# One-hot moves of 16 rows, and transposes of three more head pairs on VectorE and DMA, in a fused attention and feed-forward kernel

## The chip, the cores and the metric

The kernel runs on one core of a Trainium2 chip (trn2). The metric is the device time of one execution in microseconds (us). Each kernel was executed several times, and medians are quoted; one of the executions was also recorded with the hardware profiler, and all lines of profiles below come from those recorded executions. An execution of a one-core kernel counts as slow when it is over 1.5% above the fastest of the same kernel; comparisons use fast runs.

Engines in the profile: PE is TensorE (matmuls; PEld its weight loads), DVE is VectorE, ACT is ScalarE, POOL is GpSimd, SP is SyncE, which only issues DMAs here (SPq is its sequencer). L220 is line 220 of the kernel that was profiled, so the same statement has other line numbers in other kernels. Of the tile names, QK are the prepared q and k, ohT the one-hot rows, S the scores, pT their exps, VX the prepared v, OB the accumulator of the output, M a bank of PSUM (the memory that TensorE writes), Tq the blocks transposed on VectorE and T the same data after it has been put in place.

## The reference

Attention with routing: every query and every key is assigned to the nearest of 16 cluster centroids of its head, and a query sees only the keys of its own cluster. The result goes through a feed-forward layer with the activation h + sin²(αh)/α.

```python
# q, k, v: (4 batches, 8 heads, 768 tokens, 64); centroids: (8, 16, 64); float32
q_assign = argmax(einsum('bhsd,hcd->bhsc', normalized(q), normalized(centroids)), -1)
k_assign = argmax(einsum('bhsd,hcd->bhsc', normalized(k), normalized(centroids)), -1)
mask = q_assign[:, :, :, None] == k_assign[:, :, None, :]
scores = where(mask, q @ k.T / sqrt(64), -1e9)
attn = softmax(scores)
x = (attn @ v) as (3072 tokens, 512)
h = x @ w_in                       # (512, 2048)
g = h + sin(alpha * h)**2 / (alpha + 1e-9)
out = g @ w_out                    # (2048, 512)
```

## The kernel before

The work is cut into 16 pairs of heads: pairs 0 to 3 are batch 0, and so on. For each batch, 48 attention steps (12 a pair) are followed by 16 blocks of the feed-forward layer, called the MoE stretch below. An attention step is one block of 128 keys by 768 queries of one head: two matmuls for the scores, one exp on ScalarE, and six matmuls of an earlier step's weights with V.

The mask costs no vector work: below the 64 rows of q and k lie 16 rows that hold the one-hot cluster of each token, and one row with +1 for q and −1 for k, so that a score gets an addition only within a cluster. So each pair has to be prepared in time: q and k transposed (tokens to columns), cast to bf16, multiplied by the centroids (the "cluster product", on TensorE), made one-hot on VectorE, and moved by DMA to rows 64 and up.

There are two ways to transpose. `prep_T` uses TensorE, and VectorE copies the result out. `prep_D` transposes 32×32 blocks on VectorE, and `prep_S` then places the blocks with eight DMAs of 96 KB; I call these eight a placing. Each engine gets its instructions in one fixed order; a dictionary `plan` says at which step a piece of the preparation is put into the instruction streams. The parts that matter:

```python
    NPE = 2 * NHP          # pairs 0..7 are transposed on TensorE, 8..15 by prep_D, prep_S
    ...
    def prep_S(m):         # a placing: 8 DMAs, all from SyncE's queue
        s = st[m]
        s["T32"] = trp.tile([P, 4, HS], F32, tag="T32", name="T32")   # trp has 2 buffers
        for i in range(4):
            for e in range(2):
                lo = D * (i // 2) + 32 * e
                nc.sync.dma_start(
                    out=s["T32"][lo : lo + 32, :, QS * (i % 2) : QS * (i % 2) + QS],
                    in_=s["Tq"][32 * i : 32 * i + 32, :, QS * e : QS * e + QS],
                )
    ...
    def prep_asn(m, bk=None):        # cluster product: 4 fp32 products, 8 matmul passes
        ...
        for g in range(4):
            nc.tensor.matmul(out=bk[32 * g : 32 * g + 32, 0:HS],
                lhsT=cnB[:, 2 * hp + g // 2, :], rhs=s["T32"][:, g, :], start=True, stop=True)
    ...
    def prep_move(m):                # one-hot rows and the sign row: 17 rows
        ...
            nc.sync.dma_start(
                out=QK[D:KR, m % NQK, h, t],
                in_=s["ohT"][32 * g : 32 * g + NHC + 1].rearrange("c a n -> c (a n)"),
            )
    ...
    def prep(m, s0):
        if m == 1:
            s0 -= 4
        else:
            for g in range(4):
                if m < NPE:
                    if m != NHP + 3 or g == 3:
                        at(s0 + g, lambda g=g: prep_T(m, g))
                else:
                    at(s0 - 5 + g, lambda g=g: prep_D(m, g))
            if m >= NPE:
                at(s0 - 2, lambda: prep_S(m))
                s0 += STEPS          # STEPS is 12: the consumers come a pair later
            at(s0 + 2, lambda: prep_cast(m, 0))     # GpSimd
            at(s0 + 4, lambda: prep_cast(m, 1))
        at(s0 + 5, lambda: (prep_asn(m), prep_hot(m, 0)))
        at(s0 + 6, lambda: (prep_hot(m, 1), prep_hot(m, 2)))
        at(s0 + 7, lambda: (prep_hot(m, 3), prep_move(m)))
    # ... weights of the MoE: GpSimd issues these 512 KB loads in its own order
    for i, fn, n in ((23, load_w_in, 0), (30, load_w_out, 0), (36, load_w_in, 1), (42, load_w_in, 2),
                     ...four more at step 47):
```

The softmax here doesn't subtract the row's maximum and nothing guards it: scores larger than these inputs give would overflow.

## Time and profile before

The median is 327.9 us (327.72 to 328.38, 3 runs). The profiled execution spans 327.7 us. The page's share of busy time, its TensorE clock and DMA rows (40 equal slices of the span, in tenths) and its DMA packets:

```profile
PE 307.2 (94%) x2744; PEld 183.0 (56%) x2787; DVE 208.0 (63%) x361; ACT 241.8 (74%) x325; POOL 112.3 (34%) x181
...
PEclk9889999999999999999999999999999999999999
DMA  7455498993016959723043948520043210000031
...
DMA packets 25298, 37.83 MB, mean 115 GB/s; under 512 B 2852, under 2 KB 19120, under 8 KB 25264
```

Batch 0 takes slices 2 to 8. The DMA row is at about half in slices 2 to 5 (8 to 41 us).

Batch 0 is 2.1 us longer than batch 1, with more TensorE work; an undisturbed exp starts 0.71 to 0.73 us after the one before, so 48 of them would take about 35 us. The timeline of TensorE in batch 0 shows the work that the change is about (start, duration, engine, line, operation):

```profile
43.55 0.52 PE L143 MATMUL M<-ident_f,k 128*128 128x128 f32 x3
...
45.27 0.85 PE L211 MATMUL M<-T,cnB 128*32 128x384 f32 x8
```

The first is one of the transposing groups of `prep_T`, the second a cluster product: it makes its step about 1.4 us long.

In the first MoE stretch TensorE waits a little for the output weights, and over the whole execution GpSimd waits long for placings (total us, times, longest):

```profile
PE OB L360 <- DMA w_out_bf<-in_moe_w_out_dram: 0.7, 2, 0.3
...
POOL QK L190 <- DMA T<-Tq: 88.6, 10, 30.8
```

### The profile page before, as it was taken

To read this page: it belongs to the slowest core of one execution; us is meant where nothing else is said; L and a number is where in the kernel's file an instruction comes from. 1 tells how busy PE (TensorE), PEld (TensorE's weight loads), DVE (VectorE), ACT (ScalarE), POOL (GpSimd) and SP (SyncE) were. 2 spreads that over 40 slices of the span, in tenths; PEclk is the share of its full clock that TensorE was granted. 3 is DMA by queue.
4 is the path that set the end of the run, shared out by engine and by line. 5 is a ranking of instruction groups with operands and counts; after the bars stand their busy time and mean duration, and the time that the engine had idled before them with its cause. 6 is when DMAs were issued, how large, how long until landed. Compare 5 with 4: busy or idle time off the path is not lost.

```text
span 327.7 us, 7166 instructions
## 1 busy us (share of the span) xinstructions
PE 307.2 (94%) x2744; PEld 183.0 (56%) x2787; DVE 208.0 (63%) x361; ACT 241.8 (74%) x325; POOL 112.3 (34%) x181
## 2 busy tenths in 40 slices
PE   6699999899999999999999998999999999999995
PEld 3266665555555655555555565655555666555544
DVE  4578887487837556587837766677836613577721
ACT  5288888777678988687778887787779899688300
POOL 7858787620007069280005366340006200000000
PEclk9889999999999999999999999999999999999999
DMA  7455498993016959723043948520043210000031
GB/s 230 139 174 167 137 201 184 209 215 108 10 64 181 233 108 247 222 61 132 2 116 93 233 108 245 143 85 2 0 113 88 60 44 34 0 35 0 0 127 67
DMA packets 25298, 37.83 MB, mean 115 GB/s; under 512 B 2852, under 2 KB 19120, under 8 KB 25264
## 3 DMA queue, kind: packets, MB, share of 16 engines
q0 software_dynamic: 8704, 19.93, 24.0%
q1 hardware_dynamic: 16346, 17.39, 18.6%
q8 instruction: 22, 0.36, 0.5%
q14 instruction: 12, 0.10, 0.1%
q10 hardware_dynamic: 214, 0.06, 0.1%
HBM read 27.30 MB, written 6.29 MB: 103 GB/s over the span
## 4 chain that ended last, share of the span: by engine, by line
PE 56%; DMA 15%; DVE 7%; ACT 7%; POOL 5%; issue 4%; SPq 3%; ACTq 0%; POOLq 0%; DVEq 0%
PE S L389 14%; PE M L360 11%; PE S L313 7%; DMA w_out_bf<-in_moe_w_out_dram 7%; ACT pT L319 6%; PE M L389 6%; DMA k<-in_k_dram 4%; PE OB L328 4%; PE OB L360 4%; DMA T<-Tq 4%; PE S L314 3%; PE M L211 3%; PE S L360 2%; SPq L175 2%; POOL QK L185 2%
## 5 line engine op out<-in xcount | busy, mean ns | idle before, releaser
L319 ACT ACTIVATE pT<-S 128x768 bf16<-128x768 f32 x192 | 145.3, 810 | 27.4 <-PE S L314 25.0
L360 PE MATMUL M<-w_out_bf,gT 128*128 128x512 bf16 (+1 forms) x259 | 82.1, 372 | 0.6 <-DVE asT L243 0.3
L313 PE MATMUL S<-QK 81*128 81x512 bf16 x192 | 73.7, 384 | 7.1 <-POOL QK L185 3.4
L389 PEld LDWEIGHTS <-w_in_bf 128*128 128x128 bf16 x512 | 49.6, 98 | 38.6 <-issue 2.8
L328 PEld LDWEIGHTS <-pT 128*128 128x128 bf16 x1152 | 55.7, 98 | 24.6 <-DVE xs L340 3.5
L389 PE MATMUL S<-xT,w_in_bf 128*128 128x512 bf16 (+1 forms) x348 | 65.0, 325 | 1.1 <-DVE gT L409 0.5
L190 POOL TENSOR_SCALAR QK<-T 64x384 bf16<-64x384 f32 x64 | 33.3, 520 | 94.2 <-DMA T<-Tq 88.6
L328 PE MATMUL OB<-VX,pT 128*128 128x65 bf16 x1152 | 61.0, 194 | 1.9 <-DVE xs L340 1.8
L400 ACT ACTIVATE s_sb<-S,alpha_col 128x768 bf16<-128x768 f32 x44 | 39.4, 902 | 25.3 <-PE S L389 16.2
L360 PEld LDWEIGHTS <-gT 128*128 128x128 bf16 x400 | 39.0, 98 | 28.2 <-issue 2.0
L314 PE MATMUL S<-QK 81*128 81x256 bf16 x192 | 52.2, 272 | 0.0
L409 DVE SCALAR_TENSOR_TENSOR gT<-u_sb,ralpha,S 128x768 bf16<-128x768 bf16 x44 | 44.5, 1013 | 11.2 <-ACT u_sb L405 8.3
L185 POOL CAST QK<-T 64x768 bf16<-64x768 f32 x32 | 26.5, 829 | 43.8 <-DVE T L149 35.9
L314 PEld LDWEIGHTS <-QK 81*128 81x128 bf16 x192 | 18.9, 99 | 22.2 <-issue 7.7
L389 PE MATMUL M<-xT,w_in_bf 128*128 128x512 bf16 (+1 forms) x156 | 29.7, 324 | 0.7 <-DVE gT L409 0.5
L407 DVE TENSOR_TENSOR u_sb<-s_sb 128x768 bf16<-128x768 bf16 x40 | 23.7, 593 | 8.5 <-ACT s_sb L400 8.3
L313 PEld LDWEIGHTS <-QK 81*128 81x128 bf16 x192 | 18.8, 98 | 16.2 <-issue 11.2
L339 DVE RECIPROCAL rec<-OB 128x6 f32<-128x6 f32 x32 | 5.9, 186 | 32.9 <-PE OB L328 32.9
L400 ACT ACTIVATE s_sb<-M,alpha_col 128x512 bf16<-128x512 f32 (+1 forms) x40 | 21.0, 575 | 7.8 <-PE M L389 7.8
L409 DVE SCALAR_TENSOR_TENSOR gT<-u_sb,ralpha,M 128x512 bf16<-128x512 bf16 (+1 forms) x40 | 22.8, 611 | 5.9 <-ACT u_sb L405 5.4
L360 PE MATMUL OB<-w_out_bf,gT 128*128 128x512 bf16 (+1 forms) x76 | 24.6, 356 | 0.7 <-DMA w_out_bf<-in_moe_w_out_dram 0.7
L405 ACT ACTIVATE u_sb<-s_sb 128x768 bf16<-128x768 bf16 x24 | 20.2, 843 | 0.8
(82 smaller groups left out, 262.5 us busy)
## 6 DMA issues: line engine op xcount, KB each, us to landing
T<-Tq SPq DMA_DIRECT2D x64, 96.0 KB
out_dram<-o_sb SPq DMA_DIRECT2D x23, 256.0 KB
v<-in_v_dram POOLq DMA_DIRECT2D x14, 384.0 KB, 4.8
q<-in_q_dram POOLq DMA_DIRECT2D x13, 384.0 KB, 6.0
k<-in_k_dram POOLq DMA_DIRECT2D x13, 384.0 KB, 6.8
w_in_bf<-in_moe_w_in_dram POOLq DMA_DIRECT2D x4, 512.0 KB, 11.8
w_out_bf<-in_moe_w_out_dram POOLq DMA_DIRECT2D x4, 512.0 KB, 18.8
QK<-ohT SPq DMA_DIRECT2D x60, 25.5 KB
```

The source lines that it names most:

```text
L185: nc.gpsimd.tensor_copy(out=QK[0:D, m % NQK, h, :, HS * par : HS * par + HS], in_=src)
L190: nc.gpsimd.tensor_scalar(out=QK[0:D, m % NQK, h, t].rearrange("c (n i a) -> c i n a", i=4, a=32)[:, 2 * par : 2 * par + 2], in0=src[:, t] ...
L313: nc.tensor.matmul(out=dst[:, 0:512], lhsT=lhsT, rhs=T[:, 0, 0:512], start=True, stop=True)
L314: nc.tensor.matmul(out=dst[:, 512:S], lhsT=lhsT, rhs=T[:, 0, 512:S], start=True, stop=True)
L319: nc.scalar.activation(out=pT, in_=area(i)[:, 0:S], func=ACTF.Exp, scale=escale)
L328: nc.tensor.matmul(out=o3[:, j, :], lhsT=pT[:, P * j : P * j + P], rhs=VX[m % NVX][:, h, jof(m // NHP, kt), :], start=(kt == 0 and j == 0) ...
L360: nc.tensor.matmul(out=bk[:, lo:hi], lhsT=gT[:, f, P * mt : P * mt + P], rhs=w_out_bf[:, f, lo:hi], start=(f == 0), stop=(f == NF - 1),)
L389: nc.tensor.matmul(out=ar[lo // 512][:, 0 : hi - lo] if isinstance(ar, tuple) else ar[:, lo:hi], lhsT=lhsT, rhs=xT[:, kk, lo:hi], start=(k ...
L400: nc.scalar.activation(out=s_sb[:, lo:hi], in_=src, func=ACTF.Sin, scale=alpha_col[:, f : f + 1])
L405: nc.scalar.activation(out=u_sb, in_=s_sb, func=ACTF.Square)
L407: nc.vector.tensor_tensor(out=u_sb, in0=s_sb, in1=s_sb, op=ALU.mult)
L409: nc.vector.scalar_tensor_tensor(out=gT[:, f, lo:hi], in0=u_sb[:, lo:hi], scalar=ralpha[:, f : f + 1], in1=src, op0=ALU.mult, op1=ALU.add,)
```

## The change

Its intent: (1) move 16 one-hot rows instead of 17, with the constant sign row written once, so that the DMA can be spread over all 16 DMA engines; (2) take the transposes of pairs 4 to 6 off TensorE in batch 0, the costliest attention stretch; (3) halve the cluster products of batch 0 over two steps; (4) put VectorE's pieces one to a step, away from the steps in which it must free the output accumulator; (5) issue the loads of q and k for pairs 8 to 10 in the first MoE, behind a small copy ("pacer") that waits for a point in the MoE. The core of the diff:

```diff
-    NPE = 2 * NHP
+    NPE = NHP
+    MIX = NHP + 3                       # pair 7: still on TensorE, in the first MoE
...
             nc.sync.dma_start(
-                out=QK[D:KR, m % NQK, h, t],
-                in_=s["ohT"][32 * g : 32 * g + NHC + 1].rearrange("c a n -> c (a n)"),
+                out=QK[D : D + NHC, m % NQK, h, t],
+                in_=s["ohT"][32 * g : 32 * g + NHC].rearrange("c a n -> c (a n)"),
             )
...
+    for t in range(2):                  # sign rows, once, in the prologue
+        nc.sync.dma_start(
+            out=QK[D + NHC : KR, :, :, t, :].rearrange("c s h n -> c (s h) n"),
+            in_=sgn[:, t, :].unsqueeze(1).to_broadcast([1, 2 * NQK, S]),
+        )
...
+    def hot_steps(m, a):
+        asn_at.add(a)
+        if a < ASTEPS:
+            at(a - 1, lambda: prep_asn(m, 0, 2))
+            at(a, lambda: (prep_asn(m, 1, 2), prep_hot(m, 0)))
+        else:
+            at(a, lambda: (prep_asn(m), prep_hot(m, 0)))
+        at(a + 1, lambda: prep_hot(m, 1))
+        at(a + 2, lambda: prep_hot(m, 2))
+        at(a + 3, lambda: (prep_hot(m, 3), prep_move(m)))
...
+    def prep_new(m, k0):
+        for g, d in enumerate((-10, -9, -7, -6)):
+            at(k0 + d, lambda g=g: prep_D(m, g))
+        at(k0 - 5, lambda: prep_S(m))
+        at(k0 + 5, lambda: prep_cast(m, 0))
+        at(k0 + 6, lambda: prep_cast(m, 1))
+        hot_steps(m, k0 + 8)
...
+    for m, k0 in {4: 24, 5: 33, 6: 42}.items():
+        prep_new(m, k0)
+    for m, i in {3: 0, 4: 0, 5: 8, 6: 16, 7: 40}.items():
+        at(i, lambda m=m: load_qk(m, eng=nc.gpsimd))
...  # pairs 8 and up: prep_new(m, ASTEPS * b + STEPS * n)
...  # v loads of pairs 5 and up: 26 steps ahead instead of 14
...  # output matmuls of the MoE, used as filler, keep out of all product steps
+            if b == 0 and f == 8:
+                nc.gpsimd.tensor_copy(out=pacer, in_=gT[0:1, f - 2, 0:1])
+                for m in late:
+                    load_qk(m, eng=nc.gpsimd)
```

## The prediction

> **What bounds it now.** The page gives PE 94% busy, ACT 74%, DVE 63%. By the starts of the exps (timeline, ScalarE) I cut the 327.7 us into: prologue 14.1; attention of the four batches 44.6, 42.5, 43.0, 40.3; the MoE stretches after the first three 32.1, 31.5, 31.0; the last MoE and output 48.8. The MoE pitch is 1.73 us per 128 hidden units: TensorE-bound, not to be had. In attention the floor is ScalarE: exps that wait for nothing start every 0.71 to 0.73 us, 48 x 0.72 = 34.6 us a batch. Batch 0 lies 10 us above it:
> - a step with three fp32 transposes (L143) has a pitch of 0.87, 0.15 over the floor; 20 of them, about 3 us;
> - a step with a cluster product (L211, eight matmuls, 0.78 to 0.85 us) takes about 1.4, 0.7 over; six, about 4 us;
> - the rest: PV waiting for VectorE to free OB (one step of 1.66 us, one of 1.27), first steps, x transposes.
>
> **One-hot moves.** The Trainium skill (DMA: Bandwidth & Descriptors, Queues, rings and completion order) says that a copy is spread over the largest number of engines up to 16 that divides its outer size; 17 rows go to one. The trace agrees: such a move leaves 17 packets and one 4-byte completion packet, a 128-partition load 16. The moves issued at 58 to 61 us trickle until about 79 us; DMA share falls from 1.2 to 0.1 at 76 us, yet the last weights land at 81.4 and 83.9: one engine lags. Sixteen rows remove that. In the prologue, moves of 34 packets (0.65 us each, serial) end just before the first scores (13.55 us): I expect these 0.5 to 1 us earlier.
>
> **Pairs 4 to 6.** 36 of batch 0's transposes go. VectorE is even (twelve 0.54 us transposes for twelve 0.55 us evacuations). GpSimd casts grow from 3.3 to 4.2 us a pair. Placing adds 3 x 0.77 MB, about 3.7 us of 16 engines each (packets of 768 B, 58 ns). Loads come earlier, and the DMA was half idle from 16 to 40 us, so weights should not be later than now.
>
> **Halved products.** 0.43 us fits a step's slack; about 0.35 saved on each of four pairs. Pair 6's product moves to batch 1, which gets five instead of three.
>
> **Later batches.** New places avoid the step in which VectorE frees OB: steps of 1.46 to 1.53 should become 0.9, those of 1.34 about 1.06, of 1.74 to 1.80 about 1.4. Batch 3 has one product less, and takes three more output matmuls.
>
> **Sum (estimates from these durations), us saved:** prologue 0.7; batch 0 4.2 (to 40.4); first MoE 0.6 (weight waits of 0.66 and a load wait of 0.35 go, one more transposing group of 0.36 comes); batch 1 0.4; second MoE 0.4; batch 2 1.7; batch 3 0.9; end 0.5. Together 9.4; I take off 0.9 for new VectorE and GpSimd queues in batch 0 (80 to 90% busy there by these counts). Nearly all is on the critical path, as ScalarE idles there.
>
> **Predicted: 319.4 us**, 8 times in 10 within 315.5 to 324.0. Chances: faster by over 2% 0.72, within 2% 0.26, slower 0.02.
>
> **Right if** batch 0's exps span 39 to 42 us, no MoE matmul waits for weights, moves show 16 completion packets, the tail at 76 to 84 us is gone, batch 2 spans about 41. **Wrong if** the first MoE waits for w_out or w_in (placing and loads collide), if PV in batch 0 waits over a microsecond for OB, or GpSimd, blocked on a placing, issues weights late. Then only batches 2 and 3 gain: about 324.

One correction to its wording: the rule for the number of engines stands, in the Trainium skill's page "DMA: Bandwidth & Descriptors", in the section "Why a DMA increments its semaphore by 16 and not by 1", not in the section that the prediction names.

## More of the kernel before

Note for later that a pair that is placed by DMA had its placing at step `s0 - 2` and its cast and product at `s0 + 14` and `s0 + 17`: 16 and 19 steps behind.

The span cut at the exps that begin and end each attention stretch. Columns are: window, its length, busy us (and instructions) of PE, PEld, DVE, ACT and POOL, then the granted TensorE clock, the DMA share and GB/s. The lines are batch 0, the first MoE, batch 1 and batch 2:

```profile
14.11:58.66 44.55, 41.79 (x501) 27.95 (x503) 33.90 (x64) 37.12 (x48) 34.43 (x45) 0.96 0.66 170
58.66:90.79 32.13, 29.98 (x183) 16.98 (x185) 23.61 (x34) 23.38 (x33) 5.56 (x8) 1.00 0.64 127
90.79:133.24 42.45, 40.56 (x464) 24.95 (x472) 24.64 (x49) 36.22 (x48) 21.88 (x34) 1.00 0.65 170
...
164.71:207.69 42.98, 41.14 (x469) 24.66 (x477) 27.90 (x54) 35.97 (x48) 19.67 (x34) 1.00 0.63 163
```

The same cut for 16 to 40 us, and from 41 us to the end of batch 0, shows a DMA share of 0.49 and then 0.91:

```profile
16.00:40.00 24.00, 22.61 (x275) 15.67 (x274) 19.68 (x38) 19.50 (x26) 16.73 (x23) 0.96 0.49 150
41.00:58.66 17.66, 16.39 (x207) 11.20 (x206) 13.22 (x25) 15.10 (x20) 14.89 (x20) 1.00 0.91 198
```

## The result, and the profile after

The changed kernel takes 338.53 us (median of 4 runs, 337.31 to 339.68) against 327.81 (4 runs) before. The ratio is 1.033 (95% interval 1.029 to 1.037): slower. Ratios here and below are the mean time of one kernel's fast runs over that of the other's of the same rounds, so they are not quite the ratio of the medians. The results were correct.

The same parts of the page, after:

```profile
PE 308.8 (92%) x2742; PEld 181.8 (54%) x2783; DVE 205.5 (61%) x360; ACT 242.9 (72%) x326; POOL 116.8 (35%) x188
...
PEclk9989978999999996999999999999999999999999
DMA  7464968989733586592105385632011000000022
...
DMA packets 29746, 40.14 MB, mean 119 GB/s; under 512 B 4264, under 2 KB 23568, under 8 KB 29712
```

The clock row has two dips that were not there, in slices 6 and 7 and in slice 16. The packets under 512 B rise by 1412, from 2852 to 4264: a move leaves 16 completion packets now instead of one (1028 of the rise, as a run below shows), and the other 384 are 16 for each of the 24 DMAs of the three new placings. The stages (batch 0, first MoE, batch 1, batch 2, as before):

```profile
14.35:62.26 47.91, 40.78 (x489) 26.42 (x489) 29.99 (x60) 36.96 (x48) 31.40 (x47) 0.89 0.76 188
62.26:94.50 32.24, 29.95 (x186) 17.16 (x188) 23.19 (x34) 23.76 (x34) 18.26 (x27) 1.00 0.95 224
94.50:143.67 49.17, 43.91 (x478) 25.48 (x485) 31.32 (x59) 36.56 (x48) 23.08 (x38) 0.93 0.55 141
...
174.66:217.89 43.23, 40.68 (x470) 24.43 (x477) 29.00 (x55) 36.27 (x48) 17.31 (x31) 1.00 0.57 139
```

Batch 0 has lost one us of TensorE work and is 3.36 us longer; batch 1 is 6.72 us longer. These two make 10.1 us of a difference of 9.2 in the spans; the other stages differ by half a us or less. So the loss has to be found in two places, and TensorE's timeline shows the first:

```profile
41.97 0.27 PE L327 MATMUL S<-QK 81*128 81x256 bf16 x1
42.07 0.35 PE L341 MATMUL OB<-VX,pT 128*128 128x65 bf16 x6
45.55 0.53 PE L220 MATMUL M<-T,cnB 128*32 128x192 f32 x8 [3.13 <-DMA T<-Tq]
46.02 0.39 PE L326 MATMUL S<-QK 81*128 81x512 bf16 x1
...
47.30 0.87 PE L220 MATMUL M<-T,cnB 128*32 128x192 f32 x8 [0.78 <-DMA T<-Tq]
48.09 0.61 PE L326 MATMUL S<-QK 81*128 81x512 bf16 x1
```

The bracket is the idle time before an instruction and what ended it. The first half product of pair 4 comes up 8.5 us after the first issue of that pair's placing (42.42 and 33.91 us) and waits 3.13 us for it, and the scores of the next step stand behind it in TensorE's order. The next product takes 0.87 us instead of 0.53, and the scores 0.61 instead of 0.39: the clock is at half from 46.4 to 53.3 us.

When was the placing issued, and why does it land so late? First SyncE's issues, then GpSimd in the same time:

```profile
33.91 5.67 SPq L176 DMA_DIRECT2D T<-Tq  x8
39.67 5.06 SPq L300 DMA_DIRECT2D QK<-ohT  x4
```

```profile
35.40 0.77 POOL L615 DMA_DIRECT2D w_in_bf<-in_moe_w_in_dram  x1
44.37 1.07 POOL L197 TENSOR_SCALAR QK<-T 64x384 bf16<-64x384 f32 x2 [8.20 <-DMA QK<-ohT]
47.33 3.66 POOL L197 TENSOR_SCALAR QK<-T 64x384 bf16<-64x384 f32 x6 [1.89 <-DMA T<-Tq]
51.05 0.81 POOL L621 DMA_DIRECT2D w_out_bf<-in_moe_w_out_dram  x1
```

Eight issues take 5.67 us. Beside them go the loads of q, k and v that GpSimd issued just before, and 512 KB of w_in, issued at 35.40. The fourth of the eight lands at 44.21, the last at 47.16: 13.3 us after the first was issued. GpSimd, at its cast, is held 8.2 us and then again, and the load of w_out that stands behind it, planned for step 30 (whose exp starts at 41.59), goes out at 51.05. (The profile names a one-hot move as what ended the 8.2 us; the fourth block, which that cast needs, landed at 44.21, so the named releaser is a bystander.) SyncE is held too: its fourth one-hot move goes out at 44.22, 2.7 us after it was done with the third. In all these runs SyncE's DMAs share eight semaphores, and this one waits for the semaphore of the fourth block, which landed at 44.21: so it is the program's semaphores that let no more than eight of SyncE's DMAs be unfinished. The chain of waits that ended last runs, in this stretch, from the last block's landing to GpSimd's cast; two of its pieces:

```profile
38.83 8.33 DMA T<-Tq
...
47.33 0.51 POOL QK L197
```

The second place, in batch 1, has the same form. Pair 9's placing is issued at 113.82, the loads of q, k and v of later pairs between 116.72 and 118.94, and the eighth block lands at 125.99, 12.2 us after the first issue. The product comes up at 122.9, 9.1 us after the first issue:

```profile
113.82 6.07 SPq L176 DMA_DIRECT2D T<-Tq  x8
...
126.45 1.51 PE L220 MATMUL M<-T,cnB 128*32 128x384 f32 x8 [3.58 <-DMA QK<-ohT]
```

(Here too the named releaser is a bystander: TensorE's sequencer passes its wait for the eighth block's semaphore at 126.02, and needs until 126.45 for the checks of the other seven.)

Placings with few such neighbours in the same trace are faster: pair 5's took 7.6 us to its last landing (first issue at 44.91), and so did pair 8's (104.53). TensorE's waits at the cluster product, in whose releasers the landings of placings and of one-hot moves are mixed as above:

```profile
PE M L220 <- DMA T<-Tq: 5.0, 3, 3.1
PE M L220 <- DMA QK<-ohT: 4.4, 2, 3.6
```

### The profile page after: what moved, and what is told of

It reads as the page before. It is cut to its first block, busy times and chain, and to the rows that moved or that the text cites. A ratio compares the mean times of both kernels' runs of the same rounds, so it can differ in the third digit from the quotient of the medians.

```text
span 336.9 us, 7217 instructions
## 1 busy us (share of the span) xinstructions
PE 308.8 (92%) x2742; PEld 181.8 (54%) x2783; DVE 205.5 (61%) x360; ACT 242.9 (72%) x326; POOL 116.8 (35%) x188
## 2 busy tenths in 40 slices
DMA packets 29746, 40.14 MB, mean 119 GB/s; under 512 B 4264, under 2 KB 23568, under 8 KB 29712
## 4 chain that ended last, share of the span: by engine, by line
PE 61%; DMA 14%; SPq 8%; ACT 4%; DVE 4%; POOL 4%; issue 3%; POOLq 0%; DVEq 0%; ACTq 0%
PE S L402 16%; PE M L373 12%; PE S L326 7%; PE M L402 7%; SPq L176 7%; DMA T<-Tq 6%; PE OB L341 5%; PE OB L373 5%; DMA q<-in_q_dram 4%; DMA QK<-ohT 4%; POOL QK L197 3%; PE S L327 3%; ACT pT L332 3%; PE S L373 2%; PE M L220 2%
## 5 line engine op out<-in xcount | busy, mean ns | idle before, releaser
L373 PE MATMUL M<-w_out_bf,gT 128*128 128x512 bf16 (+1 forms) x262 | 83.4, 373 | 0.2
L326 PE MATMUL S<-QK 81*128 81x512 bf16 x192 | 75.5, 394 | 7.5 <-DMA QK<-ohT 2.8
L197 POOL TENSOR_SCALAR QK<-T 64x384 bf16<-64x384 f32 x88 | 46.4, 527 | 95.2 <-DMA T<-Tq 68.3
L341 PEld LDWEIGHTS <-pT 128*128 128x128 bf16 x1152 | 58.3, 100 | 23.3 <-issue 3.5
L402 PE MATMUL S<-xT,w_in_bf 128*128 128x256 bf16 (+1 forms) x345 | 64.8, 325 | 0.5
L341 PE MATMUL OB<-VX,pT 128*128 128x65 bf16 x1152 | 62.8, 197 | 0.3 <-DVE xs L353 0.3
L402 PE MATMUL M<-xT,w_in_bf 128*128 128x256 bf16 (+1 forms) x154 | 29.4, 324 | 0.3
L326 PEld LDWEIGHTS <-QK 81*128 81x128 bf16 x192 | 19.0, 99 | 15.0 <-issue 10.1
L209 POOL CAST VX<-v 128x768 bf16<-128x768 f32 x16 | 14.4, 901 | 33.6 <-PE OB L341 32.7
L373 PE MATMUL OB<-w_out_bf,gT 128*128 128x512 bf16 (+1 forms) x79 | 25.8, 357 | 0.0
L220 PE MATMUL M<-T,cnB 128*32 128x384 f32 (+1 forms) x152 | 14.6, 458 | 10.4 <-DMA T<-Tq 5.0
## 6 DMA issues: line engine op xcount, KB each, us to landing
w_in_bf<-in_moe_w_in_dram POOLq DMA_DIRECT2D x4, 512.0 KB, 10.1
```

The costliest lines, as they stand in the source:

```text
L197: nc.gpsimd.tensor_scalar(out=QK[0:D, m % NQK, h, t].rearrange("c (n i a) -> c i n a", i=4, a=32)[:, 2 * par : 2 * par + 2], in0=src[:, t] ...
L220: nc.tensor.matmul(out=s["asn"][32 * g : 32 * g + 32, w * part : w * part + w], lhsT=cnB[:, 2 * hp + g // 2, :], rhs=s["T32"][:, g, w * pa ...
L326: nc.tensor.matmul(out=dst[:, 0:512], lhsT=lhsT, rhs=T[:, 0, 0:512], start=True, stop=True)
L341: nc.tensor.matmul(out=o3[:, j, :], lhsT=pT[:, P * j : P * j + P], rhs=VX[m % NVX][:, h, jof(m // NHP, kt), :], start=(kt == 0 and j == 0) ...
L373: nc.tensor.matmul(out=bk[:, lo:hi], lhsT=gT[:, f, P * mt : P * mt + P], rhs=w_out_bf[:, f, lo:hi], start=(f == 0), stop=(f == NF - 1),)
L402: nc.tensor.matmul(out=ar[lo // 512][:, 0 : hi - lo] if isinstance(ar, tuple) else ar[:, lo:hi], lhsT=lhsT, rhs=xT[:, kk, lo:hi], start=(k ...
```

## The experiments

**Theory A (latency).** A placing takes 7 to 8 us alone and 10 to 16 us beside loads. The change made its consumers come 10 to 13 steps behind it, and TensorE, GpSimd and SyncE each stand still when they meet a placing that has not landed (3.1, 8.2 and 2.7 us above). **Rival B (more DMA work).** The three additional placings are simply too much for the DMA in batch 0, wherever the consumers stand, and weights come late. **Rival C.** Something else of the change costs the time: the halved products, the new places of VectorE's work, or the 16-row moves.

The expectations use other letters. Their theories A (too few steps) and B (loads beside the placing), later A+B, are the two halves of theory A here; their theory C (traffic as such) is rival B here; their theory D (16-row moves are dearer) is a part of rival C here.

All kernels below gave correct results. Each was run in three rounds with the kernel before on the same chip. "Batch 0" and so on are the lengths of the stages in the profiled run.

### First set: consumers later, loads elsewhere, and the moves alone

**Consumers of the product later.** The product and what follows it go six steps back, except for pair 6; the casts stay.

```diff
-    trp = ctx.enter_context(tc.tile_pool(name="trp", bufs=2))
+    trp = ctx.enter_context(tc.tile_pool(name="trp", bufs=3))
...
-        hot_steps(m, k0 + 8)
+        hot_steps(m, k0 + (8 if m == 6 else 14))
```

> The cluster products and the one-hot chain of pairs 4, 5 and 8 to 15 start six steps later (and T32 has three buffers); nothing else moves. Theory A (the product stands only 13 steps behind the issue of its placing, TensorE takes its work in order, and so it stands still until the placing has landed; the half clock follows the standstill): the steps of 4.3 and 2.4 us in batch 0 and of 5.8 us in batch 1 go, so do both stretches of half clock; batch 0 about 41.5, batch 1 about 41.5, batch 2 about 41.5, in all 320 to 325 us. Theory C (the loss is the larger DMA traffic or the heavier VectorE and GpSimd queues as such, wherever the product stands): the stall only moves, 334 us or more. Theory D (16-row moves are dearer): no change, about 338.

Measured: 337.67 us, ratio 1.022 (1.014 to 1.030). One of the four runs, and it is the profiled one, counts as slow by the rule (339.84 with a fastest of 334.24), so its trace is used here only for where it waits. The product of pair 4 no longer waits, but three others do:

```profile
47.24 0.61 PE L326 MATMUL S<-QK 81*128 81x512 bf16 x1 [1.46 <-DMA QK<-ohT]
...
67.70 0.90 PE L144 MATMUL M<-ident_f,q 128*128 128x128 f32 x3 [3.48 <-DMA q<-in_q_dram]
...
208.18 0.82 PE L341 MATMUL OB<-VX,pT 128*128 128x65 bf16 x12 [2.22 <-POOL VX L209]
```

The scores of pair 3 wait for its one-hot moves, which stand behind pair 4's placing on SyncE's queue. The MoE waits for pair 7's q: GpSimd issues that load, and was held at a cast. In batch 2, V's cast comes late for the same reason. So one late placing holds three queues, and moving one consumer only moves the wait.

**Loads apart from placings.** The weight loads go behind the casts of pair 4, and the loads of later q, k and v away from the placing of pair 9.

```diff
-        (23, load_w_in, 0), (30, load_w_out, 0), (36, load_w_in, 1), (42, load_w_in, 2),
+        (41, load_w_in, 0), (42, load_w_out, 0), (43, load_w_in, 1), (45, load_w_in, 2),
...
-   at(ASTEPS * b + (-26, -3, -2, -1)[n], lambda m=m: load_qk(m, eng=nc.gpsimd))
+   at(ASTEPS * b + (-19, -3, -2, -1)[n], lambda m=m: load_qk(m, eng=nc.gpsimd))
...
-   at(max(0, STEPS * m - (14 if m < 5 else 26)), lambda m=m: load_v(m, nc.gpsimd))
+   at(max(0, STEPS * m - (14 if m < 5 else 26 if m < 8 else 19)), lambda m=m: load_v(m, nc.gpsimd))
```

> The products stay where the change put them; only loads move away from the placings: w_in 0 and w_out 0 from steps 23 and 30 to 41 and 42, w_in 1 and 2 to 43 and 45, the q and k loads of pairs 11 and 15 and the later v loads seven steps later. Theory A alone (13 steps are too few in any case): the stalls stay, about 336 us. Theory B (a placing needs 13 steps or fewer when nothing else uses the DMA engines; it is late because a load was issued beside it): both large stalls shrink to under 1 us, about 322 to 327 us; weights may then be late in the first MoE, by at most 3 us. Theory D: no change.

Measured: 338.73 us, ratio 1.030 (1.024 to 1.037), no gain in all, but the stalls are gone where they were: pair 4's placing lands in 9.8 us, pair 9's in 7.5, batch 0 is 43.27 us (from 47.91), and the stalled step of batch 1 falls from 5.84 to 1.25 us. The price is paid elsewhere: the MoE waits for its weights, and a later step of batch 1 takes 4.21 us, behind the next placing, pair 10's, which took 11.8.

```profile
PE S L402 <- DMA w_in_bf<-in_moe_w_in_dram: 6.9, 1, 6.9
```

The first MoE is 40.13 us instead of 32.24. This supports theory A on what delays a placing, and part of rival B too: batch 0 has to load weights *and* place, and the two compete for the time before the MoE.

**The kernel before with 16-row moves.**

```diff
-                out=QK[D:KR, m % NQK, h, t],
-                in_=s["ohT"][32 * g : 32 * g + NHC + 1].rearrange("c a n -> c (a n)"),
+                out=QK[D : D + NHC, m % NQK, h, t],
+                in_=s["ohT"][32 * g : 32 * g + NHC].rearrange("c a n -> c (a n)"),
...  # and the same in the prologue's moves, and the sign rows as in the change
```

> The kernel before with one part of the change alone: one-hot moves of 16 rows, the sign row written once. If 17 rows on one DMA engine hold back the weights (the reason in the prediction): waits of MoE matmuls for weights of 0.7 us go and the last weights land several us earlier, in all 0.5 to 1.5 us faster than before, about 326.8. If the moves matter to nothing critical: 327.8 within 0.3. Theory D (16 rows are dearer): slower by over 1 us.

Measured: 326.26 us, ratio 0.992 (0.987 to 0.997): a small gain that the interval resolves. The DMA line of its page against that of the kernel before:

```profile
DMA packets 26290, 37.78 MB, mean 116 GB/s; under 512 B 3880, under 2 KB 20112, under 8 KB 26256
```

The bytes are nearly the same and the small packets rise by 1028; 16 completion packets instead of one on 68 moves make 1020 of them (68 × 15). The last weights land at 75.2 us instead of 83.9, the first MoE falls from 32.13 to 31.15 us, batch 0 from 44.55 to 43.18. The fall of batch 0 is not the work of the moves: it lies in the first steps (1.80 and 1.08 us became 0.83 and 0.69), which the profiled run of the kernel before had at half clock and this one had not. The first exp comes at 14.63, not earlier but 0.5 us later than before. This part of the change is no part of the loss.

**The change with 17-row moves**, the counterpart (the moves and sign rows as before, all else as after):

> The changed kernel with moves of 17 rows again and no sign row. Theory D: it gains most of the 10 us back, about 329. Theories A and B: the stalls stay or get worse, since one engine is slower with everything that all sixteen must finish: 338 to 345 us.

Measured: 341.89 us (336.49 to 343.86). Three of its four runs lie over 1.5% above the fastest and count as slow, so no ratio can be given. In the profiled one (slow) the first MoE takes 37.81 us and the last weights land at 88.6. The direction agrees with the experiment before; no number is drawn from it beyond that. Its first exp comes at 13.57 us, 0.8 earlier than with the sign rows.

### Second set: undo the parts

**Pairs 4 to 6 back on TensorE**, at the steps of the kernel before; all else as in the change.

```diff
+    MIXES = range(NHP, NHP + 4)
...
-    for m, s0 in {1: 0, 2: 4, 3: 12, MIX: ASTEPS + 2}.items():
+    for m, s0 in {1: 0, 2: 4, 3: 12, 4: 20, 5: 28, 6: 36, MIX: ASTEPS + 2}.items():
         prep(m, s0)
-    for m, k0 in {4: 24, 5: 33, 6: 42}.items():
-        prep_new(m, k0)
-    for m, i in {3: 0, 4: 0, 5: 8, 6: 16, 7: 40}.items():
+    for m, i in {3: 0, 4: 6, 5: 14, 6: 22, 7: 40}.items():
```

> The changed kernel with pairs 4 to 6 transposed on TensorE again, at the places they had before (their products in halves); all else as changed. Theory A+B (a placing lands late because it shares the DMA engines with loads, and whatever waits for it in order stands still: the product on TensorE, the casts on GpSimd and behind them the loads, the next moves on the DMA queue): with no placings in batch 0 its stall and half clock go, batch 0 about 42 to 43 us; batch 1 keeps a stall of several us at the product of pair 9 or 10; in all 327 to 333 us. Theory C (traffic as such): similar in batch 0, and batch 1 without a stall, since less traffic is left over: 322.

Measured: 327.29 us, ratio 0.994 (0.989 to 1.000). The median is 11.2 us under the changed kernel's, as much as the change had lost (10.7). Batch 0 is 43.84 us and batch 1 43.57, the last weights land at 76.7. So rival C falls for everything but the new path of pairs 4 to 6 and what their places do to batch 1. Batch 1 has some stalls left (steps of 2.22, 1.72 and 1.75 us). That these are shorter than in the changed kernel is not fully explained by one cause: casts and product of pair 6 also left batch 1.

**The same, and the consumers of pairs 8 and up later** (casts at `k0 + 12` and `+ 13`, product at `k0 + 14`, three buffers in `trp`):

> As the run before, and the casts and products of pairs 8 to 15 stand 17 and 19 steps behind the issue of their placing, as before the change, where the change has 10 and 13. Theory A+B: no step of batches 1 to 3 over 1.5 us but the first, no half clock; batch 1 about 41.5, batch 2 about 41.5, in all 320 to 324 us, the first kernel here that beats the one before by more than 1%. If the slack is not what matters: stalls stay, 327 or more.

Measured: 328.20 us, ratio 0.997 (0.992 to 1.003). No gain; a miss. Batches 1 and 2 are both 43.62 us. The stalls are at other steps: in batch 2 the longest, 2.22 us, is a product that waits for a PSUM bank which VectorE frees when it copies an output tile out. The product had moved onto that step.

**The kernel before with 16-row moves and halved products.** Halves at `s0 + 4` and `s0 + 5` for pairs 2 to 6:

```diff
-        at(s0 + 5, lambda: (prep_asn(m), prep_hot(m, 0)))
+        if 1 < m and s0 + 5 < ASTEPS:
+            at(s0 + 4, lambda: prep_asn(m, 0, 2))
+            at(s0 + 5, lambda: (prep_asn(m, 1, 2), prep_hot(m, 0)))
+        else:
+            at(s0 + 5, lambda: (prep_asn(m), prep_hot(m, 0)))
```

> The kernel before with 16-row moves and the cluster products of pairs 2 to 6 in halves, nothing else. By the prediction's count a halved product saves 0.35 us, on five pairs 1.7 us of batch 0: 324.5 us. If VectorE, not the product, holds these steps: no gain over 16 rows alone, 326.3.

Measured: 328.37 us, ratio 0.997 (0.991 to 1.004): no gain, a miss. Batch 0 is 46.49 us instead of the 43.18 without halves. At four of the five places the step of the first half takes 1.60 us (1.41 at the other): it stands directly behind the last transpose of its pair and waits for VectorE to copy that out. Another part is in the first steps, which this run had at half clock (3.4 us of it, none in the run without halves). Where a step lies between, as in the two experiments before, halves do no harm, but save nothing either: the two steps of pair 2's halves take 1.12 and 1.08 us, 2.20 together, against 0.71 before and 1.45 for the whole product, 2.16 together, in the kernel with 16-row moves alone. So rival C is right on a small point: the halves have no gain to give here.

**The change with everything later, as far as its deadlines allow** (casts of pairs 4 and 5 at `k0 + 11`, product at `k0 + 14`; pair 6 at +7 and +10; others +12 and +14; the weights at steps 30, 36, 38 and 43; three buffers in `trp`):

> The changed kernel with its placings in batch 0 kept, but every consumer later: casts of pairs 4, 5 and 8 to 15 six or seven steps later and products six (pair 6 two), and the first two weight loads six or seven steps later. Theory A+B: batch 0 about 41 us without a step over 2 us, the later batches as in the run with late consumers, in all 319 to 325 us. Theory C: the traffic does not fit before the first MoE, so a wait of several us comes up there or in batch 0: 327 or more.

Measured: 332.46 us (one of the four runs, 335.0, counts as slow), ratio 1.007 (0.999 to 1.015), in the median 6 us under the change. Batch 1 is 42.44 us again (from 49.17), so its loss was the distance. Batch 0 stays at 47.73: the scores of pair 3 wait 2.66 us for one-hot moves that stand behind the placing on SyncE's queue.

### Third set: more distance

**Pairs 4 to 6 on TensorE, and the consumers of the others 22 to 25 steps behind the placing** (from 10 and 13):

```diff
-    trp = ctx.enter_context(tc.tile_pool(name="trp", bufs=2))
+    trp = ctx.enter_context(tc.tile_pool(name="trp", bufs=3))
...
-        at(k0 + 5, lambda: prep_cast(m, 0))
-        at(k0 + 6, lambda: prep_cast(m, 1))
-        hot_steps(m, k0 + 8)
+        at(k0 + 17, lambda: prep_cast(m, 0))
+        at(k0 + 18, lambda: prep_cast(m, 1))
+        hot_steps(m, k0 + 20)
```

> Pairs 4 to 6 on TensorE; pairs 8 to 15 keep the change's places within the period of twelve steps (transposes, products and one-hot steps away from the steps in which VectorE frees OB), but casts and products come one whole period later, 23 and 25 steps behind the issue of the placing. Theory A+B: no waits for placings, so the change's better places pay at last: batches 1 and 2 about 41.5 us each against 42.5 before; in all 322 to 324.5 us, 1 to 2% faster than before. If the places pay nothing, 326.

Measured: **324.67 us, ratio 0.989 (0.985 to 0.994)**, the fastest kernel, faster than both the kernel before and the change, though by less than 2%. Batch 0, first MoE, batch 1 and batch 2:

```profile
14.37:58.34 43.97, 42.62 (x541) 29.19 (x541) 33.19 (x64) 37.35 (x48) 33.10 (x44) 0.96 0.69 178
58.34:89.78 31.44, 29.38 (x183) 16.95 (x185) 23.49 (x33) 23.65 (x33) 14.09 (x19) 1.00 0.87 196
89.78:132.15 42.37, 40.61 (x465) 24.68 (x473) 26.60 (x51) 36.18 (x48) 20.86 (x35) 1.00 0.68 178
162.70:204.10 41.40, 40.70 (x470) 24.36 (x477) 29.04 (x55) 36.27 (x48) 18.47 (x32) 1.00 0.65 154
```

Batch 2 is 41.40 us instead of 42.98 before: with the distance kept, the new places of VectorE's work are worth what was expected of them. Product steps take 1.21 us (1.40 before), and the steps that took 1.46 us at VectorE's collisions take 0.91. One step of batch 1 still takes 2.22 us. Against the kernel before with 16-row moves alone (0.992), the lead is within the intervals.

**The change with pairs 4 to 6 later and wider spread:** placing points `k0` at 30, 36 and 42 (from 24, 33, 42), casts and product at +8 and +11 (pair 6 +7 and +10), the others +17 and +20, three buffers each in `trp` and `tqp`; a warm-up tile was cut from 640 to 512 columns.

> As the run before for pairs 8 to 15, but with pairs 4 to 6 by VectorE transposes and placings as in the change, spread and later: transposes six steps apart from step 20 on, behind the moves of pair 3, casts 13 and products 16 steps behind the placing's issue (pair 6 in batch 1), loads of weights where the change has them. Theory A+B (the change's idea is sound, its slack too small): no stall over 1.5 us in batch 0, batch 0 about 40.5, in all 320 to 323, better than with TensorE transposes. Theory C (the placings' traffic does not fit into batch 0 together with the weights): waits of several us in batch 0 or the first MoE, 325 or more.

Measured: 331.57 us, ratio 1.011 (1.005 to 1.017). Batches 1 and 2 are 41.79 and 41.13 us, lower than in any kernel so far. Batch 0 is 50.73, with one step of 8.23 us: pair 4's placing, in the middle of the weight loads, takes 15.0 us and the product waits 5.8.

**Sign rows from ScalarE's queue,** in the kernel before with 16-row moves, to win back the prologue: `nc.scalar.dma_start` directly after the centroids' load, with the constant made on VectorE.

> The kernel before with 16-row moves; the sign rows are made by VectorE and written from ScalarE's queue at the start, not from the SP queue ahead of the first one-hot moves. If the two sign DMAs on the SP queue hold the first moves back: first exp 0.5 to 1 us earlier than the 14.6 us with the sign rows on SP; in all 325.3 to 326. Else 326.3.

Measured: 330.96 us, ratio 1.010 (1.005 to 1.014). A miss: the first exp comes at 18.74 us instead of 14.63. ScalarE's own work stands behind the two DMAs and starts at 7.04 us instead of 1.19; the profile counts the idle time from the start of the span:

```profile
ACT L482 <- DMA QK<-sgn: 7.0, 1, 7.0
```

### Last set: is it the weights?

**The kernel with a wider spread, and its weights paced away from the first placing** (w_out and the second part of w_in at step 39, the third at 45):

> As the run with spread VectorE transposes, but w_out 0 and w_in 1 stand on GpSimd's queue behind the cast of pair 4, so behind the landing of its placing, and w_in 2 behind that of pair 5. If the order of loads is all that was wrong: batch 0 about 41 us, no wait for weights over 1 us, in all under 323. If placings and weights do not both fit: batch 0 and the first MoE together stay over 75.5 us (76.7 before the change, 74.3 with 16-row moves alone), by waits in either; in all 324 to 329.

Measured: 330.90 us, ratio 1.007 (1.002 to 1.012). Pair 4's placing takes 11.3 us instead of 15.0, batch 0 falls from 50.73 to 45.75, and the first MoE rises from 32.59 to 37.94, where TensorE waits for pair 7's q:

```profile
PE M L144 <- DMA q<-in_q_dram: 4.0, 2, 3.6
```

Batch 0 and first MoE together are 83.7 us, against 83.3 without the pacing, 76.7 in the kernel before, and 75.4 with pairs 4 to 6 on TensorE (the kernel of 324.67 us).

**All weights first.** The change with its eight weight loads issued in the prologue. It cannot be fast, as the loads of q and k have to share the DMA with all the weights, but from about 35 us on there is no weight on the way any more.

```diff
     for i in range(NVX):
         nc.gpsimd.memset(VX[i][:, :, :, D : D + 1], 1.0)
+    for n in range(4):
+        load_w_in(n)
+        load_w_out(n)
     load_qk(1)
...
-    for i, fn, n in ((23, load_w_in, 0), (30, load_w_out, 0), ... ):
-        at(i, lambda fn=fn, n=n: fn(n))
```

> The changed kernel with all eight weight loads issued first of all, in the prologue; batch 0 starts later for it, which is not the question. If the weight loads are what holds the placing of pair 4: its last landing within 9 us of its first issue (13.2 in the changed kernel), and the two steps of 4.3 and 2.4 us at its product shrink to under 2.5 us together; the stall in batch 1, which is beside q, k and v loads, stays (over 4 us). If the placing's own issue and queues hold it: both stalls stay as they are.

Measured: 343.66 us, ratio 1.046 (1.042 to 1.051), slow for the reason given: one early step takes 7.03 us, as it waits for pair 3's q. At the place in question, however, pair 4's placing lands in 8.2 us instead of 13.3, and its first half product does not wait. The loads of q, k and v are beside it as in the change (issued from 43.81 to 46.04 us here, from 32.42 to 34.68 there), so it is the weights that are missing:

```profile
54.11 0.35 PE L341 MATMUL OB<-VX,pT 128*128 128x65 bf16 x6
54.39 0.53 PE L220 MATMUL M<-T,cnB 128*32 128x192 f32 x8
54.86 0.39 PE L326 MATMUL S<-QK 81*128 81x512 bf16 x1
```

The two steps take 1.08 and 0.89 us, where they took 4.28 and 2.40. Batch 1's stall, where q, k and v loads are the neighbours, is left as it was: 5.03 us (5.84 in the change). That is the cleanest separation: the weights make the stall of batch 0, and not that of batch 1, which fell from 5.84 to 1.25 us when the loads of q, k and v were moved as well.

## Why the prediction was wrong

It expected 319.4 us and gave a slowdown a chance of 2%; it is 338.5. Stage by stage in the profiled runs:

| stage | expected change, us | measured, us |
|---|---|---|
| prologue | −0.7 | +0.24 |
| batch 0 | −4.2 | +3.36 |
| first MoE | −0.6 | +0.11 |
| batch 1 | −0.4 | +6.72 |
| second MoE | −0.4 | −0.48 |
| batch 2 | −1.7 | +0.25 |
| batch 3 | −0.9 | −0.27 |
| last MoE and output | −0.5 | −0.53 |
| allowance for queues | +0.9 | in the above |

**The step that failed** is this one of the paragraph on pairs 4 to 6: "Placing adds 3 x 0.77 MB, about 3.7 us of 16 engines each ... Loads come earlier, and the DMA was half idle from 16 to 40 us, so weights should not be later than now." It costs a placing as an amount of work and compares that with a mean share. What the critical path sees is the time from first issue to last landing, which is another quantity: 7.6 us alone, 13.3 beside weights, 12.2 beside loads of q, k and v. The mean itself was right (a share of 0.49 from 16 to 40 us), but it covers only the start of the time in question: from 41 to 58.66 us the kernel before had the DMA engines at 0.91 already, and the three placings were issued at 33.91, 44.91 and 54.29. Over the whole run the work grew by only 6% (37.83 MB to 40.14). The prediction did not compare that time with the distance to the consumer, which the diff shrinks from 16 to 10 steps for the cast and from 19 to 12 or 13 for the product. Ten undisturbed steps are about 7.2 us (10 × 0.72): less than a placing takes alone.

The Trainium skill had what was needed to see it. "DMA: Bandwidth & Descriptors", section "Issuing engines are not separate DMA queues", says that DMAs of all issuing engines run on the same 16 DMA engines and interleave; "Queues, rings and completion order" adds that an engine takes turns between its queues packet by packet. The trace agrees with the sharing: a placing from SyncE's queue is stretched by loads from GpSimd's queue, from 7.6 to 13.3 us. That the turns go by packets no run here shows.

**One late landing, three queues.** "I take off 0.9 for new VectorE and GpSimd queues" was the second mis-sized term. The placing holds TensorE at the product (3.13 us and 0.78), GpSimd at the cast (8.2 us and 1.89, with the next weight load behind it), and SyncE's next one-hot moves (2.7 us). The list of what would make it wrong named GpSimd "blocked on a placing", but as a reason for late weights; TensorE's own product, in order before the next scores, was not on it. The weights did come later (the last at 85.0 us instead of 83.9), but the first MoE did not wait for them in the changed kernel; that expectation held.

**Then the clock.** After TensorE's waits of 3.13 and 3.58 us the clock is at half for 6.8 us each, and for 17.1 us in all in the changed kernel (3.4 before). The skill's page "TensorE: Matmul & The Clock Gate", section "What's actually happening", describes a free-running window of 3413 ns and half clock after an idle one. All stretches of half clock in these traces, but those cut off by the end of a run, are multiples of 3.41 us, which agrees. The windows before them were not idle, though: TensorE was busy for 0.87 and 1.35 us of the 3.41 (the first figure after the length; the clock is the third from the right):

```profile
43.01:46.42 3.41, 0.87 (x10) 0.30 (x10) 0.23 (x1) 0.13 (x1) 1.01 (x2) 1.00 0.51 89
121.52:124.93 3.41, 1.35 (x15) 0.59 (x11) 0.92 (x3) 2.26 (x4) 0.00 (x0) 1.00 0.95 233
```

How much of the loss is the clock's own was not measured apart. An estimate from the steps that only the clock slows, counted from 0: steps 33 to 36 of batch 0 take 4.21 us instead of 2.90 in the run with all weights first, and steps 33 and 34 of batch 1 take 3.13 instead of 1.64 in the fastest kernel, 2.8 us together of the 10.1.

**Batch 0, estimated without its stall.** Steps 31 to 36 hold the stall and the half clock behind it. They take 10.89 us in the changed kernel and 4.87 in the run with all weights first; with the latter, batch 0 would take about 41.9 us (an estimate from these durations), between the expected 40.4 and the 44.55 before. So much of the gain on TensorE is there and was outweighed. Could it be had? In this schedule I did not find it: batch 0 and first MoE together were 80.2 us in the changed kernel, 79.6 with everything later, 83.3 with the placing moved, 83.7 with the weights paced as well and 83.4 with loads apart, against 76.7 before and 75.4 with these pairs on TensorE. The weights must be in by the MoE, and three placings want the same 30 us. Whether another order of loads would do stays open.

**What was right.** The reasoning on the moves: 16 rows go over 16 engines, and the section "Why a DMA increments its semaphore by 16 and not by 1" of the DMA page is borne out (3880 small packets instead of 2852, last weights 8.7 us earlier, the first MoE 1 us shorter). The second MoE and the end came as expected, the former with the moves alone too (30.77 us from 31.47). The new places of VectorE's work were right too, but the shrunken distance took the gain of batch 2 away: −1.58 us (42.98 to 41.40) once the consumers were late again, where −1.7 was expected. Of batch 3's −0.9 only −0.27 came.

**What was wrong besides.** The prologue was expected 0.7 us shorter. The two sign-row DMAs are on SyncE's queue in front of the first moves and take it until 9.35 us:

```profile
6.17 3.19 SPq L475 DMA_DIRECT2D QK<-sgn  x2
```

SyncE's first one-hot move is issued at 9.66 us, 0.85 later than in the kernel before (8.81). The prediction counted the moves that become faster and not the two new DMAs in front of them; in the run without them the first exp came at 13.57 us. And the halves, expected to save 0.35 a pair, saved nothing (2.20 us for two steps against 2.16), and cost something where their input was not ready a step earlier.

## What to carry to other kernels

Cost a DMA that feeds an in-order engine as time from first issue to last landing, with the traffic that will be beside it, and compare that with the distance in steps to its first consumer; free bandwidth on average says nothing of it. When a change moves a producer to a DMA, look for every queue in which someone waits for it, as each of them also holds what stands behind. If a change bundles several parts, try them apart: here the moves alone gained 0.8%, and moves, places and loads together, without the new path for pairs 4 to 6 and with the consumers far enough behind, gained 1.1%, while the bundle lost 3.3%.

## What the Trainium skill lacked or had wrong

- "DMA: Bandwidth & Descriptors", "Bandwidth": its table of measured times is for single HBM→SBUF copies issued from GpSimd. It has no row for a set of small SBUF→SBUF copies from one queue, where the issue counts. Here eight copies of 96 KB took 7.1 to 7.6 us from first issue to last landing alone, of which 5.5 to 6.0 us are the issues (most of them 0.60 to 0.63 each), and 10 to 16 us beside loads on another queue.
- The same page, "Issuing engines are not separate DMA queues": it calls the issuing time on the sequencer "usually small relative to the DMA itself". For these copies it was not: 0.6 us of some 2.2 from the issue of one copy to its landing, and for the eight in a row 5.5 to 6.0 us of 7.1 to 7.6.
- "TensorE: Matmul & The Clock Gate", "What's actually happening": half clock is said to follow an idle window of about 3.4 us. Here no idle window was needed: TensorE was busy for 0.87 and 1.35 us in the windows before the two stretches of the changed kernel, and for 1.76 us in the one before 52.00 us of the run with paced weights, where the longest wait was 1.61 us.
